# Starting the first query chunks on one token tile, with one reused transposing bank and the key weights loaded earlier

## The chip, the cores and the metric

The kernel runs on one core of a Trainium2 chip. The metric is the device time of one execution in microseconds (us). A profile accompanies every execution timed here: it gives the span (first to last instruction) and the mean granted TensorE clock, and for one execution per run a whole trace. Times in the traces are counted from the start of the span. "Fast" executions are those not marked as disturbed.

Engine names in the profile: PE is TensorE's matmuls, PEld its weight loads, DVE VectorE, ACT ScalarE, POOL GpSimd, SP SyncE. A small q after a name is that engine's sequencer or queue.

## The reference

Two layers, each an attention block A and a feed-forward block B, both with a residual, over 2048 tokens of width 1024 in bf16:

```python
x = A_x
for layer in range(2):               # written out twice in the original
    x = x + A(layernorm(x), wqkv, wo)        # 32 heads; token s attends to s, s-2, ..., s-14
    x = x + B(layernorm(x), w1, b1, w2, b2)  # gelu(x @ w1 + b1) @ w2 + b2, width 3584
```

(Condensed.) Only the first few steps matter here: the layernorm of the first 512 tokens (four tiles of 128), its transposition, and the first product, the queries `q = layernorm(x) @ Wq`.

## The kernel before

The kernel works on groups of 512 tokens. `qkv_chunk` computes 128 of the 1024 output columns for a group: eight matmuls (k = 0 to 7), each with a 128x128 piece of weights, whose columns are taken at a stride of eight (`c::NCH`), against up to 512 token columns. `acc_tile()` hands out one of the eight PSUM banks. In the traces the matmuls come in program order (after the change: 14 weight matmuls, 8 transposes, 42 weight matmuls, and so on as in the code), so a matmul that waits holds up those behind it.

The start loads tiles 0 and 1 of x, then the query weights in four pieces of two k each (512 KB), with x tiles 2 and 3 between them:

```python
load_x(0, 0, 2)
wq_first = [wpool.tile([P, KD // 2, D], BF16, name="wt") for _ in range(2)]
for k in range(0, KD, 2):
    load_wq_piece(wq_first[k // (KD // 2)], k)
    if k < 4:
        load_x(0, 2 + k // 2, 3 + k // 2)
```

Meanwhile TensorE runs warm-up matmuls on zeros. The layernorm of the first two tiles, and their transposition on TensorE (eight 128x128 transposes into a bank, then copies to SBUF), come as a pair:

```python
def ln_first():
    ...
    stats(0)
    stats(1)
    xn0 = norm(0)
    xn1 = norm(1)
    transpose_on_pe(xn0, xa[0][:, 0, :, :], parts=[act.copy] * 4)
    ps = transpose_bias()
    transpose_on_pe(xn1, xa[0][:, 1, :, :], parts=[vec.tensor_copy] * 2 + [act.copy] * 2)
    warm_up(2)
    act.copy(b1T[:], ps[:])
    stats(2)
    stats(3)
    for tt in range(2, 4):
        first_late.append((norm(tt), xa[0][:, tt, :, :]))
    ...
```

Then seven query chunks run over tiles 0 and 1 (256 columns), a quarter of the k at a time; the transposes of tiles 2 and 3 are put in between, and all chunks then take their other 256 columns:

```python
for kq in range(4 if n == 0 else 0):
    for c in range(7):
        first[c] = qkv_chunk(wq, c, xnT, first.get(c), kq * (KD // 4), (kq + 1) * (KD // 4), 0, 2)
        if (kq, c) == (2, 3):
            transpose_on_pe(*first_late.pop(0))
        if (kq, c) == (3, 4):
            ...
            transpose_on_pe(*first_late.pop(0))
            act.hold()
```

The layernorms of groups 1 and 2 (`ln_early`, eight tiles) follow on VectorE before its first attention products. The main program begins:

```python
warm_up(14)
ln_first()
build_constants()
with tc.tile_pool(name="early", bufs=1) as early:
    load_x(1)
    load_x(2)
    stage(gen_qkv(0, qk_next=early), sides=at(14, load_b2))
    ...
```

Of the kernel before, what the change touches and what calls it, by code (L numbers as in the profile page):

```python
# [17 lines left out]
def kernel(  # L18
# [18 lines left out]
    P = 128  # L37
# [100 lines left out]
    wq_first = [wpool.tile([P, KD // 2, D], BF16, name="wt") for _ in range(2)]  # L138
    for k in range(0, KD, 2):
        load_wq_piece(wq_first[k // (KD // 2)], k)  # L140
        if k < 4:
            load_x(0, 2 + k // 2, 3 + k // 2)

    warm = bigp.tile([P, P], BF16, name="big")
    vec.memset(warm[:], 0.0)
# [33 lines left out]
    def transpose_bias():  # L179
        ps = psum.tile([P, KF], BF16, name="acc", bufs=8)  # L180
        pe(nc.tensor.transpose(ps[:], b1_rows[:], ident[:KF, :KF]))  # L181
        return ps


    def ln_stats(t, mv=None, rstd=None):
        stats = lnp.tile([P, 2, 6], F32, name="stats")
# [7 lines left out]
        pool.tensor_tensor(out=rstd[:], in0=rstd[:], in1=mhalf[:], op=ALU.pow)  # L194
        return mv, rstd

    def ln_stats_ahead(g):
        junk = lnp.tile([P, D], BF16, name="xn", bufs=3)
        for tt in range(NTT):
            t, mean, var = g * NTT + tt, mv_ahead[:, tt, 0:1], mv_ahead[:, tt, 1:2]  # L200
            less = lnp.tile([P, 1], F32, name="less")
            act.activation(junk[:], x[t][:], ACT.Identity, scale=-1.0 / D, accum_out=less[:])
            act.activation(junk[:], x[t][:], ACT.Square, bias=less[:], accum_out=var)
            pool.tensor_scalar(out=mean, in0=less[:], scalar1=-1.0, scalar2=None, op0=ALU.mult)
            rstd = rstd_ahead[:, tt, :]
            pool.tensor_scalar(out=rstd, in0=var, scalar1=1.0 / D, scalar2=EPS, op0=ALU.mult, op1=ALU.add)
            pool.tensor_tensor(out=rstd, in0=rstd, in1=mhalf[:], op=ALU.pow)

    def ln_norm(t, mv, rstd, xn=None):
        if xn is None:  # L210
# [1 line left out]
        vec.tensor_scalar(out=xn[:], in0=x[t][:], scalar1=mv[:, 0:1], scalar2=rstd[:], op0=ALU.subtract, op1=ALU.mult)  # L212
        return xn

    def transpose_on_pe(xn, out, parts=None):
        pst = psum.tile([P, KD, P], BF16, name="acc", bufs=8)
        for k in range(KD):
            pe(nc.tensor.transpose(pst[:, k, :], xn[:, k * P:(k + 1) * P], ident[:]))  # L218
        parts = parts or [act.copy]
        n = KD // len(parts)  # L220
        for h, copy in enumerate(parts):
            copy(out[:, h * n:(h + 1) * n, :], pst[:, h * n:(h + 1) * n, :])
# [5 lines left out]
        xn = ln_norm(t, mv, rstd)  # L228
        last_transpose[0] = sp.dma_start_transpose(xnT[:, tt, :, :], xn[:].rearrange("s (k p) -> s k p", p=P))

    first_late = []

    def ln_first():

        xa[0] = new_xnT()
        vec.on = act.on = True
        mvs = {}
        stds = {}

        def stats(tt):  # L240
            st6 = lnp.tile([P, 2, 6], F32, name="stats")
            for h in range(2):
                vec.bn_stats(st6[:, h, :], x[tt][:, h * HALF:(h + 1) * HALF])
            mvs[tt] = lnp.tile([P, 2], F32, name="mv")
            vec.bn_aggr(mvs[tt][:], st6[:])
            stds[tt] = lnp.tile([P, 1], F32, name="std")
            act.activation(stds[tt][:], mvs[tt][:, 1:2], ACT.Sqrt, bias=eps_t[:])

        def norm(tt):
            rstd = lnp.tile([P, 1], F32, name="rstd")  # L250
            vec.reciprocal(rstd[:], stds[tt][:])
            return ln_norm(tt, mvs[tt], rstd)

        stats(0)
        stats(1)
        xn0 = norm(0)
        xn1 = norm(1)
        transpose_on_pe(xn0, xa[0][:, 0, :, :], parts=[act.copy] * 4)
        ps = transpose_bias()
        transpose_on_pe(xn1, xa[0][:, 1, :, :], parts=[vec.tensor_copy] * 2 + [act.copy] * 2)  # L260
        warm_up(2)
        act.copy(b1T[:], ps[:])
        stats(2)
        stats(3)
        for tt in range(2, 4):
            first_late.append((norm(tt), xa[0][:, tt, :, :]))
        vec.on = act.on = False
        act.hold()

    def new_xnT(pool=None):  # L270
        return (pool or xnp).tile([P, NTT, KD, P], BF16, name="xnT")
# [7 lines left out]
    xa = {}  # L279
    xb = {}  # L280

    def qkv_chunk(wts, c, xnT, ps=None, k0=0, k1=KD, t0=0, t1=NTT):
        if ps is None:
            ps = acc_tile()
        for k in range(k0, k1):
            mm(ps[:, t0 * P:t1 * P], lhsT=wts[k // (KD // 2)][:, k % (KD // 2), c::NCH], rhs=xnT[:, t0:t1, k, :],
               start=(k == 0), stop=(k == KD - 1), skip_group_check=t1 - t0 < NTT)
        return ps

    def add_prods(n):  # L290
# [13 lines left out]
            for _ in range(1 if c == 1 else 2):  # L304
                add_prods(n)

    def gen_qkv(n, defer=False, qk_pool=None, v_late=False, qk_next=None, v_first=False, mix=0):
        g = n % NG
        xnT = xa.pop(n)
        s = st[n]  # L310
        s["prods"] = []
        qk_pool = qk_pool or attp
        if v_first:
            wv = load_qkv(2)
        wq = wq_first if n == 0 else load_qkv(0)
        if not v_first:
            wk = load_qkv(1)

        def values():
            vT = attp.tile([P, NCH, HALO + T], BF16, name="vT", bufs=2)  # L320
            s["vT"] = vT
            act.on = n > 2
            act.copy(vT[:, :, 0:HALO], (zhalo if g == 0 else vhalo)[:])
            act.on = False
            for c in range(NCH):
                ps = qkv_chunk(wv, c, xnT)
                act.copy(vT[:, c, HALO:], ps[:])
                yield
            if g + 1 < NG:
                act.copy(vhalo[:], vT[:, :, T:T + HALO])  # L330

        if v_first:
            yield from values()
            wk = load_qkv(1)
        if n == 0:
            early_tiles = ln_early((1, None), (2, qk_next))
            for _ in range(NTT):
                next(early_tiles)
            wv = load_qkv(2)
            for _ in early_tiles:  # L340
                pass
            load_x(3)
        qT = qk_pool.tile([P, NCH, T], BF16, name="qT")
        first = {}
        for kq in range(4 if n == 0 else 0):
            for c in range(7):
                first[c] = qkv_chunk(wq, c, xnT, first.get(c), kq * (KD // 4), (kq + 1) * (KD // 4), 0, 2)
                if (kq, c) == (2, 3):
                    transpose_on_pe(*first_late.pop(0))
                if (kq, c) == (3, 4):  # L350
                    for done in range(2):
                        act.copy(qT[:, done, 0:2 * P], first[done][:, 0:2 * P])
                    transpose_on_pe(*first_late.pop(0))
                    act.hold()
        if n == 0:
            first[7] = qkv_chunk(wq, 7, xnT, t0=0, t1=2)
        for c in list(first)[2:]:
            act.copy(qT[:, c, 0:2 * P], first[c][:, 0:2 * P])
        kT = qk_pool.tile([P, NCH, HALO + T], BF16, name="kT")
        s["qT"], s["kT"] = qT, kT  # L360
        act.on = n > 2
        act.copy(kT[:, :, 0:HALO], (zhalo if g == 0 else khalo)[:])
        act.on = False

        def query(c):
            t0 = 2 if n == 0 else 0
            ps = qkv_chunk(wq, c, xnT, t0=t0)
            act.copy(qT[:, c, t0 * P:], ps[:, t0 * P:])

        def key(c):  # L370
            ps = qkv_chunk(wk, c, xnT)
            act.copy(kT[:, c, HALO:], ps[:])
            if not defer:
                new_prod(n, c)

        ahead = mix or NCH
        turns = [(query, c) for c in range(ahead)]
        for c in range(NCH):
            turns.append((key, c))
            if ahead + c < NCH:  # L380
                turns.append((query, ahead + c))
        for i, (chunk, c) in enumerate(turns):
            if i == NCH and n > 0 and not v_late and not v_first:
                wv = load_qkv(2)
            chunk(c)
            yield
        if g + 1 < NG:
            act.copy(khalo[:], kT[:, :, T:T + HALO])
        if not v_first:
            if v_late:  # L390
                wv = load_qkv(2)
            yield from values()
# [170 lines left out]
    def ln_early(*groups):  # L563
# [5 lines left out]
            tiles += [(n * NTT + tt, xns[:, tt, :], xa[n][:, tt, :, :]) for tt in range(NTT)]  # L569
        vec.on = True  # L570
        ahead = ln_stats(tiles[0][0])
        for i, (t, xn, xT) in enumerate(tiles):
            mv_rstd = ahead
            if i + 1 < len(tiles):
                ahead = ln_stats(tiles[i + 1][0])
            ln_norm(t, *mv_rstd, xn)
            sp.dma_start_transpose(xT, xn.rearrange("s (k p) -> s k p", p=P))
            if i + 1 == len(tiles):
                vec.on = False
            yield  # L580

    def stage(gen, count=None, sides=()):

# [19 lines left out]
    hold = vec.hold  # L603

    pool.on = True
    warm_up(14)
    ln_first()
    build_constants()
    with tc.tile_pool(name="early", bufs=1) as early:
        load_x(1)  # L610
        load_x(2)
        stage(gen_qkv(0, qk_next=early), sides=at(14, load_b2))
        q1 = gen_qkv(1, defer=True, qk_pool=early, mix=NCH // 2)
        stage(q1, sides=at(0, gather, 0) + at(11, between, 0, 1) + at(11, hold) + each(av, 0, 12, 1))
        q2 = gen_qkv(2, defer=True)
# [57 lines left out]
```

## Time and profile before

| what | before | view of the profile |
|---|---|---|
| time, median of 3 | 1230.84 us (1230.77 to 1231.01) | times |
| span of the profiled execution | 1229.1 us | page |
| TensorE busy | 1221.3 us, 99% | page, part 1 |
| first statistics on x tile 0 | 3.60 us | timeline |
| first transposes | 7.19 us | timeline |
| first matmul with weights | 8.95 us | timeline |
| first key matmul | 23.87 us | matmul starts in the trace |

Part 1 of the page of before has the busy time of each engine, its share of the span and its instructions; the line below it, from part 2, is the granted TensorE clock in 40 equal slices of the span (9 is 90% or more of full speed):

```profile
PE 1221.3 (99%) x5723; PEld 632.7 (51%) x5773; DVE 864.2 (70%) x918; ACT 315.1 (26%) x507; POOL 105.2 (9%) x209
...
PEclk9999999999999999999999999999999999999999
```

TensorE is the limit: 99% busy. (It has 5723 matmul records against 5773 weight loads, because some matmul records are missing from a trace.) The chain of waits of before, followed back from the last instruction and printed in order of time (start, length, what), tells where the other 1% is:

```profile
0.73 2.85 DMA x<-in_A_x_dram
...
3.60 1.30 DVE stats L92 x2
...
4.92 0.21 DVE mv L92
5.13 1.16 DVE stats L92 x2
...
6.58 0.56 DVE xn L92
...
7.19 0.62 PE acc L218 x8
...
8.95 4.12 PE acc L117 x36
```

Up to 7.19 us the chain is not TensorE: x arrives, VectorE computes the statistics of tile 0, then those of tile 1 (the 1.16 us at 5.13), and only then normalizes tile 0. The 1.16 us are the target of the change. The timeline of PE (start, length, engine and line, operation, output and input; in brackets the idle time before and what ended it) shows the same from the side of TensorE:

```profile
0.98 5.12 PE L117 MATMUL acc<-big 128*128 128x512 bf16 x14 [0.98 <-DVE big L92]
7.19 0.62 PE L218 MATMUL acc<-ident,xn 128*128 128x128 bf16 x8 [1.09 <-DVE xn L92]
...
8.31 0.59 PE L117 MATMUL acc<-big 128*128 128x512 bf16 x2
8.95 4.12 PE L117 MATMUL acc<-xnT,wt 128*128 128x256 bf16 x36
```

From 8.95 us on TensorE does not wait, except once for about 0.2 us near 125 us: one matmul of the output projection starts 415 ns after the one before it, where 512-column matmuls are otherwise 216 ns apart, because its input oT comes late from VectorE. The timeline has the wait at the load of its weights:

```profile
125.08 11.97 PEld L117 LDWEIGHTS <-oT 128*128 128x128 bf16 x56 [0.32 <-DVE oT L92]
```

VectorE itself works almost without a break from 28 us to there. Its two longer stops in that stretch, from the timeline of DVE in before:

```profile
28.60 6.69 DVE L92 TENSOR_TENSOR big<-qT,kT 128x4096 bf16<-128x4096 bf16 x3
...
90.65 4.50 DVE L92 TENSOR_TENSOR big<-abc,vT 128x4096 bf16<-128x4096 bf16 x2 [1.98 <-DMA abc<-a]
```

The first line is where it reaches its products of queries and keys (the stop of 0.71 us is just before, for a layernorm value from GpSimd); the second is a wait of 1.98 us for a DMA.

### The profile page before, as it was taken

What the parts mean: (1) busy time and instruction counts of PE and PEld (TensorE: products, weight loads), DVE (VectorE), ACT (ScalarE), POOL (GpSimd) and SP (SyncE); (2) the same over time, 40 slices, a digit from 0 to 9 for tenths busy, and PEclk for the clock granted to TensorE, in tenths of its full rate; (3) what the DMA queues carried; (4) which work ended last, traced back from release to release, by engine and by line L of the source; (5) the groups of instructions that cost most, each with busy time, mean ns of one, the idle gap of its engine ahead of it and who ended that gap; (6) DMA issues with size and microseconds to landing.
All of it is one profiled execution on the core that took longest, in us unless ns stands there. A gap on an engine that the chain in (4) does not pass through costs nothing.

```text
span 1229.1 us, 13953 instructions
## 1 busy us (share of the span) xinstructions
PE 1221.3 (99%) x5723; PEld 632.7 (51%) x5773; DVE 864.2 (70%) x918; ACT 315.1 (26%) x507; POOL 105.2 (9%) x209
## 2 busy tenths in 40 slices
PE   9999999999999999999999999999999999999998
PEld 7666544456444564446544465444654444444444
DVE  8999896998997999375993759937599797011001
ACT  4343253014410144202441024410244001400310
POOL 3010015010101101100001000010000002000000
PEclk9999999999999999999999999999999999999999
DMA  9954674756648745856557565576664558446441
GB/s 299 293 205 154 178 238 153 201 171 206 215 133 239 188 151 167 235 169 181 155 160 233 171 171 175 155 222 202 171 199 145 189 195 203 155 160 195 154 136 52
DMA packets 220031, 226.64 MB, mean 184 GB/s; under 512 B 68194, under 2 KB 187136, under 8 KB 217920
## 3 DMA queue, kind: packets, MB, share of 16 engines
q1 hardware_dynamic: 214704, 208.69, 56.9%
q0 software_dynamic: 5264, 17.06, 3.6%
q8 instruction: 45, 0.74, 0.2%
q14 instruction: 18, 0.15, 0.0%
HBM read 189.01 MB, written 4.19 MB: 157 GB/s over the span
## 4 chain that ended last, share of the span: by engine, by line
PE 99%; DVE 0%; issue 0%; DMA 0%
PE acc L117 99%; DMA x<-in_A_x_dram 0%; DVE stats L92 0%; PE acc L218 0%; DVE xn L92 0%; DVE x L92 0%; DVE mv L92 0%; PE acc L181 0%; DVE rstd L92 0%
## 5 line engine op out<-in xcount | busy, mean ns | idle before, releaser
L117 PE MATMUL acc<-xnT,wt 128*128 128x512 bf16 (+1 forms) x3392 | 720.3, 375 | 0.1
L117 PEld LDWEIGHTS <-wt 128*128 128x128 bf16 x3392 | 400.8, 119 | 318.0 <-issue 0.5
L117 PE MATMUL acc<-wt,hT 128*128 128x512 bf16 (+1 forms) x1780 | 386.0, 376 | 2.1
L117 PEld LDWEIGHTS <-hT 128*128 128x128 bf16 x1820 | 178.1, 98 | 209.0
L92 DVE TENSOR_TENSOR big<-big 128x1024 bf16<-128x1024 bf16 (+2 forms) x184 | 244.7, 1358 | 2.2
L92 ACT ACTIVATE hT<-acc,b1T 128x512 bf16<-128x512 f32 x224 | 152.1, 687 | 325.1 <-PE acc L117 325.0
L92 DVE TENSOR_TENSOR big<-qT,kT 128x4096 bf16<-128x4096 bf16 x64 | 143.8, 2284 | 36.4 <-ACT kT L92 35.9
L92 DVE TENSOR_TENSOR tmp<-acc,b2bc 128x512 f32<-128x512 f32 x56 | 38.6, 689 | 161.6 <-PE acc L117 158.5
L92 DVE TENSOR_TENSOR big<-abc,vT 128x4096 bf16<-128x4096 bf16 x64 | 144.6, 2284 | 9.8 <-DMA abc<-a 7.4
L92 ACT CAST qT<-acc 128x512 bf16<-128x512 f32 (+1 forms) x72 | 38.2, 543 | 277.6 <-PE acc L117 277.6
L117 PE MATMUL acc<-wt,oT 128*128 128x512 bf16 x440 | 97.6, 379 | 0.5
L92 DVE BATCH_NORM_STATS2 stats<-x 128x6 f32<-128x512 bf16 x120 | 79.9, 680 | 3.7 <-DMA x<-in_A_x_dram 2.7
L117 PEld LDWEIGHTS <-oT 128*128 128x128 bf16 x448 | 43.8, 98 | 53.0 <-DVE oT L92 0.3
L92 DVE TENSOR_TENSOR x<-acc,big 128x512 bf16<-128x512 f32 (+1 forms) x9 | 5.7, 632 | 90.1 <-PE acc L117 90.0
L92 ACT CAST vT<-acc 128x512 bf16<-128x512 f32 x64 | 37.4, 585 | 100.9 <-PE acc L117 100.8
L92 POOL TENSOR_TENSOR rstd<-mv,eps_t 128x1 f32<-128x1 f32 x56 | 17.4, 311 | 527.5 <-DVE mv L92 527.5
L92 ACT CAST kT<-acc 128x512 bf16<-128x512 f32 x64 | 37.3, 585 | 68.7 <-PE acc L117 68.7
L92 DVE TENSOR_TENSOR x<-acc,x 128x512 bf16<-128x512 f32 x64 | 43.0, 672 | 4.9 <-PE acc L117 4.4
L92 DVE TENSOR_SCALAR xn<-x,mv,rstd 128x1024 bf16<-128x1024 bf16 x52 | 28.4, 546 | 19.9 <-POOL rstd L92 19.5
L92 DVE TENSOR_TENSOR x<-tmp,x 128x512 bf16<-128x512 f32 x56 | 38.6, 689 | 1.4
L92 POOL DMA_DIRECT2D big<-big x24 | 13.3, 563 | 212.8 <-DVE big L92 212.8
L92 POOL TENSOR_TENSOR rstd<-rstd,mhalf 128x1 f32<-128x1 f32 x56 | 30.9, 551 | 4.4
(63 smaller groups left out, 259.4 us busy)
## 6 DMA issues: line engine op xcount, KB each, us to landing
wt<-in_B_w_dram SPq DMA_DIRECT2D x56, 1024.0 KB, 5.8
wt<-in_B_w_dram SPq DMA_DIRECT2D x64, 896.0 KB, 4.9
wt<-in_A_wqkv_dram SPq DMA_DIRECT2D x46, 1024.0 KB, 5.7
wt<-in_A_wo_dram SPq DMA_DIRECT2D x16, 1024.0 KB, 5.3
abc<-a POOLq DMA_DIRECT2D x32, 256.0 KB, 4.7
big<-big POOLq DMA_DIRECT2D x24, 256.0 KB, 3.8
x<-in_A_x_dram SPq DMA_DIRECT2D x16, 256.0 KB, 5.7
out_dram<-x SPq DMA_DIRECT2D x31, 128.0 KB, 1.8
```

What stands on the lines that cost most here:

```text
L92: inst = f(*args, **kwargs)
L117: return pe(nc.tensor.matmul(*args, **kwargs))
```

## The change

Its intent is to fill the idle start. Tile 0 is normalized as soon as its own statistics are there, and the first query chunks begin with its 128 columns alone; tile 1 follows separately for the first four k, and from k = 4 on both run together as before. All transposes use one bank, so seven banks remain for seven chunks. The key weights Wk are queued ahead of the third group of x. Two of the eight early layernorm statistics move from VectorE to ScalarE. The bias transpose moves behind the first key chunk.

The core of the diff (cuts marked with `...`):

```diff
-        if k < 4:
-            load_x(0, 2 + k // 2, 3 + k // 2)
+        if k == 2:
+            load_x(0, 2, 4)
...
-    def ln_stats_ahead(g):
+    def ln_stats_ahead(g, t0=0):
+        act.on = g == 2
...
-    def transpose_on_pe(xn, out, parts=None):
-        pst = psum.tile([P, KD, P], BF16, name="acc", bufs=8)
+    def transpose_on_pe(xn, out, bank, parts):
+        pst = bank[:].bitcast(BF16).rearrange("p (k t) -> p k t", t=P)
...
+        bn(0, 0)
+        bn(0, 1)
+        aggr(0)
+        std(0)
+        bn(1, 0)
+        norm(0, 2)
+        bn(1, 1)
+        aggr(1)
+        transpose_on_pe(xns[0], xnT[:, 0, :, :], bank, [lambda *io: (act.copy(*io), std(1))] + [act.copy] * 3)
+        some(0, 1, 0)
+        norm(1, 2)
+        transpose_on_pe(xns[1], xnT[:, 1, :, :], bank, [vec.tensor_copy] + [act.copy] * 3)
+        some(0, 1, 1)
+        some(1, 2, 0)
+        some(1, 2, 1)
...
+        some(0, 2, 2)
+        transpose_on_pe(xns[2], xnT[:, 2, :, :], bank, [act.copy])
+        norm(3)
+        some(0, 2, 3, range(4))
+        transpose_on_pe(xns[3], xnT[:, 3, :, :], bank, [act.copy] * 4)
...
+        load_x(1)
+        s["wk"] = load_qkv(1)
+        load_x(2)
...
+        on_act = tiles[-2:]
+        tiles = tiles[:-2]
...
-    warm_up(14)
-    ln_first()
-    build_constants()
...
-        load_x(1)
-        load_x(2)
-        stage(gen_qkv(0, qk_next=early), sides=at(14, load_b2))
+        warm_up(13)
+        build_constants()
+        begin_first(early)
+        stage(gen_qkv(0), sides=at(0, transpose_bias) + at(1, ln_stats_ahead, 2, NTT - 2) + at(3, ln_end) + at(6, load_b2))
```

`some(t0, t1, kq, chunks)` runs the quarter kq of the k of seven chunks (or of those named) over tiles t0 to t1 - 1; `norm(t, 2)` normalizes in two halves.

## The prediction

> **What bounds it.** TensorE: busy 99% of the span (page, part 1), 98.8% of the chain of waits is matmuls of the one helper line, granted clock 1.00. By the timeline, matmul starts from 15.6 us on lose only about 0.2 us to waiting (at 124.7 us, for oT from VectorE, which the timeline shows working almost without a break from 28.6 us to there). So only the first 16 us can be won; the rest is 512-wide matmuls, 215.7 ns apart.
>
> **Before, the start.** Tile 0's layernorm waits for tile 1's statistics; transposes start at 7.19 us, first real matmul at 8.95, then 128 matmuls 256 wide, 109.3 ns apart (Q half chunk 0.875 us), no waits. First K matmul about 23.9 us.
>
> **What the change does, costed.**
> 1. Tile 0 alone: normalization starts about 0.8 us earlier (one statistic of 0.6 and one aggregate fewer before it), in halves. Transposes from about 6.25 us; first real matmul, after the first 0.37 us copy, at about 7.4 instead of 8.95. The two late warm-ups (0.43) go.
> 2. It adds matmuls: the first four k of tiles 0 and 1 separately, 56 of 128 columns in place of 28 of 256. Their weights are taken every 8th element, 16 bytes apart; the Trainium skill ("SBUF — State Buffer", the note on 16-byte cachelines in the section on the DMA port swizzle) says that each new line costs. The trace agrees that they are slower: strided loads take 143 ns, contiguous ones 98. A 128-wide transpose has 56 ns spacing, as the skill's N/2.4+2.5 ns gives ("TensorE: Matmul & The Clock Gate", Back-to-back issue gap); but where a strided load starts together with a transpose the next matmul comes 8 to 9 ns late. I estimate 65 ns: 42 exposed ones cost 2.7 us against 3.1 for the 28, plus 0.9 for tile 0's first fourteen, hidden in the wait for tile 1. Net +0.6 us of TensorE work.
> 3. One bank serves all transposes, so transposes wait for copies of the tile before: tile 1 about 0.2 us (ScalarE's fourth copy, about 8.4), tile 3 about 0.4 (1.01 us copy of tile 2 against 0.875 us of matmuls), then 0.15 for tile 3's last copy.
> 4. Chunk 7 is 512 wide whole: no gain. Bias transpose moves into steady state: +0.1 us.
> 5. Wk lands earlier (about 20 instead of 22 us), but TensorE did not wait for it: nothing. Weights of Q land at 6.7, 9.0, 10.8, 12.2 us, in time.
> 6. Two statistics (1.85 us each in VectorE's cadence) leave VectorE; it then waits for kT, nets about 1.2 us, and the 0.2 us wait at 124.7 goes.
>
> Sum: earlier start -1.55, work +0.6, tile 1's transposes now behind it +0.45, waits +0.75: first K matmul about 24.1 us (+0.2); bias +0.1, oT wait -0.2: about +0.1 us.
>
> **Predicted: 1230.9 us**, 1230.1 to 1231.9. Faster by over 2%: 0.01; within 2%: 0.98; slower: 0.01.
>
> **What would show it.** First x-weight matmul at 7.4; 128-wide weight matmuls 65 ns apart; waits of about 0.2 and 0.4 us before the transposes of tiles 1 and 3; first K matmul near 24.1; no oT wait near 124; no wait for Wk.
>
> **What would make it wrong.** 128-wide spacing of 56 (-0.4 us) or 100 ns (+1.5); VectorE needing more than is freed, so that the oT wait grows; ScalarE's statistics delaying kT; the sparse start letting the clock fall to half (+1 to 2 us).

## The result, and the profile after

| | median (range) of its executions | before in the same rounds | ratio of fast means |
|---|---|---|---|
| changed kernel, first measurement | 1231.95 us (1231.18 to 4648.16), 6 | 1230.95 us, 6 | 1.0007 (95%: 0.9993 to 1.002) |
| changed kernel again | 1231.08 us (1231.06 to 1231.9), 5 | 1230.81 us, 9 | 1.0003 (95%: 0.999 to 1.0017) |

A ratio is the mean time of one kernel's fast executions over that of the other's of the same rounds, so it is not quite the ratio of the medians quoted. The best estimate is a loss of 0.4 to 0.8 us, and the intervals include no loss at all.

One execution took 4648.16 us. Its trace is of the first measurement. Timeline of PE, changed kernel, slow execution:

```profile
0.98 10.76 PE L117 MATMUL acc<-big 128*128 128x512 bf16 x13 [0.98 <-DVE big L92]
11.42 2.00 PE L219 MATMUL acc<-ident,xn 128*128 128x128 bf16 x8
```

From the third warm-up on, most 512-column matmuls start 840 ns apart, the others mostly 680 (840 ns is 0.61 columns per ns, about a quarter of the 2.37 of full clock), and they never recover, while the mean granted clock is given as 1.000 for the whole span of 4646.0 us. This is not a measurement: the trace holds no clock event at all, its page has no PEclk row, and the views count time without an event as full clock. Up to there both kernels run the same program on TensorE, warm-ups on zeros, and no other of about a hundred executions did it. So it is not put down to the change. The Trainium skill ("TensorE: Matmul & The Clock Gate", section "Seeing it yourself") warns that this clock has been seen stuck at a quarter and that its records cannot be fully trusted. This trace agrees with the first by its spacing of 840 ns, and with the second in that no event tells of it.

The profile after is therefore taken from the second measurement (1231.08 us, span 1228.9 us). Part 1 of its page, and its clock:

```profile
PE 1224.2 (100%) x5790; PEld 632.6 (51%) x5790; DVE 862.4 (70%) x913; ACT 319.1 (26%) x511; POOL 111.9 (9%) x211
...
PEclk9999999999999999999999999999999999999999
```

(PE's 1224.2 us against 1221.3 before is no measure of the change: the trace of before lacks 50 matmul records.) The chain of waits after, in order of time:

```profile
0.98 5.14 PE acc L117 x13
6.12 0.57 PE acc L219 x8
...
6.71 0.37 ACT xnT L92
...
7.10 0.29 ACT std L92
7.40 0.81 ACT xnT L92 x3
...
8.25 0.61 PE acc L219 x8
8.86 4.07 PE acc L117 x56
```

The layernorm has left the chain. In its place stand the warm-ups (which in this execution end just as tile 0 becomes ready) and ScalarE's copies out of the one bank. The timeline of PE after:

```profile
5.96 0.72 PE L219 MATMUL acc<-ident,xn 128*128 128x128 bf16 x8
7.14 1.01 PE L117 MATMUL acc<-xnT,wt 128*128 128x128 bf16 x14 [0.46 <-ACT xnT L92]
8.25 0.61 PE L219 MATMUL acc<-ident,xn 128*128 128x128 bf16 x8
...
14.47 0.61 PE L219 MATMUL acc<-ident,xn 128*128 128x128 bf16 x8 [0.22 <-ACT xnT L92]
14.91 10.52 PE L117 MATMUL acc<-xnT,wt 128*128 128x256 bf16 x78
25.37 0.18 PE L181 MATMUL acc<-ident,abc 28*128 28x28 bf16 x1
```

The first weight matmul starts at 7.14 instead of 8.95 us. But the first key matmul starts at 23.55 instead of 23.87 us: of 1.81 us gained, 0.32 are left. And 0.30 of those came from x, which happened to arrive earlier (first statistics at 3.30 instead of 3.60). Counted from the first statistics, the first weight matmul comes at 3.84 instead of 5.35 us, the first key matmul at 20.25 instead of 20.27: nothing left. Counted in the same way, the start of the last matmul comes at 1222.33 instead of 1222.18 us: 0.15 us behind.

The timeline of DVE after answers for the relief of VectorE:

```profile
26.17 4.49 DVE L92 TENSOR_TENSOR big<-qT,kT 128x4096 bf16<-128x4096 bf16 x2
...
64.35 2.29 DVE L92 TENSOR_TENSOR big<-qT,kT 128x4096 bf16<-128x4096 bf16 x1 [0.92 <-ACT kT L92]
...
90.27 4.50 DVE L92 TENSOR_TENSOR big<-abc,vT 128x4096 bf16<-128x4096 bf16 x2 [2.01 <-DMA abc<-a]
```

VectorE reaches its products 2.43 us earlier (26.17 for 28.60) and is 0.38 us earlier at 90 us (90.27 for 90.65); of both, 0.30 us is again the earlier arrival of x. Between, it waited 0.92 us for a key chunk that it did not wait for before.

### The profile page after: what moved, and what is told of

Its sections match the earlier page's. It is cut to its first block, busy times and chain, and to the rows that moved or that the text cites. A ratio compares the mean times of both kernels' runs of the same rounds, so it can differ in the third digit from the quotient of the medians.

```text
span 4646.0 us, 14040 instructions
## 1 busy us (share of the span) xinstructions
PE 4641.5 (100%) x5790; PEld 1327.2 (29%) x5790; DVE 869.0 (19%) x913; ACT 322.7 (7%) x511; POOL 107.5 (2%) x211
## 4 chain that ended last, share of the span: by engine, by line
PE 100%; DMA 0%; SPq 0%; DVE 0%; issue 0%
PE acc L117 100%; DMA wt<-in_A_wqkv_dram 0%; DMA x<-in_A_x_dram 0%; PE acc L219 0%; SPq L92 0%; DVE x L92 0%; PE acc L181 0%
## 5 line engine op out<-in xcount | busy, mean ns | idle before, releaser
L117 PE MATMUL acc<-xnT,wt 128*128 128x512 bf16 (+2 forms) x3412 | 2735.6, 1084 | 0.5 <-DMA x<-in_A_x_dram 0.5
L117 PE MATMUL acc<-wt,hT 128*128 128x512 bf16 (+1 forms) x1820 | 1473.7, 1091 | 0.0
L117 PEld LDWEIGHTS <-wt 128*128 128x128 bf16 x3412 | 800.7, 236 | 1928.5 <-issue 1917.8
L117 PEld LDWEIGHTS <-hT 128*128 128x128 bf16 x1820 | 403.7, 222 | 1068.6 <-issue 1068.6
L117 PE MATMUL acc<-wt,oT 128*128 128x512 bf16 x448 | 369.8, 1104 | 0.0
L117 PEld LDWEIGHTS <-oT 128*128 128x128 bf16 x448 | 99.3, 222 | 268.7 <-issue 268.7
L92 ACT CAST qT<-acc 128x512 bf16<-128x512 f32 x64 | 37.5, 586 | 1295.2 <-PE acc L117 1295.2
L92 DVE TENSOR_SCALAR xn<-x,mv,rstd 128x1024 bf16<-128x1024 bf16 (+1 forms) x54 | 28.6, 532 | 422.1 <-DMA xnT<-xn 412.7
L117 PE MATMUL acc<-wt,qT 128*128 128x512 bf16 x64 | 52.8, 1102 | 0.0
L92 POOL DMA_DIRECT2D abc<-a x32 | 17.6, 559 | 1197.7 <-DVE a L92 1197.7
```

What stands on the lines that cost most here:

```text
L92: inst = f(*args, **kwargs)
L117: return pe(nc.tensor.matmul(*args, **kwargs))
```

## The experiments

All kernels gave correct results and were timed over five rounds (the first measurement over six executions); all traced executions but that of the first measurement were fast. Each table entry is a mean over fast executions. "After the span" is the time less the span.

| kernel | time, us | span, us | after the span, us | before, same rounds | ratio (95%) |
|---|---|---|---|---|---|
| changed, first measurement | 1231.82 | 1229.64 | 2.18 | 1231.00 | 1.0007 (0.9993 to 1.002) |
| after_again | 1231.25 | 1229.08 | 2.17 | 1230.86 | 1.0003 (0.999 to 1.0017) |
| start_only | 1232.08 | 1230.16 | 1.92 | 1230.86 | 1.001 (0.9997 to 1.0022) |
| rest_only | 1230.77 | 1228.96 | 1.81 | 1230.86 | 0.9999 (0.9987 to 1.0012) |
| warm10 | 1232.74 | 1230.58 | 2.16 | 1231.28 | 1.0012 (0.9999 to 1.0024) |
| warm16 | 1232.00 | 1229.84 | 2.16 | 1231.28 | 1.0006 (0.9993 to 1.0018) |
| bias_gap | 1231.18 | 1229.38 | 1.80 | 1231.28 | 0.9998 (0.9984 to 1.0011) |
| better | 1232.70 | 1230.90 | 1.80 | 1231.28 | 1.0011 (0.9999 to 1.0024) |
| before_w0late | 1231.18 | 1229.40 | 1.78 | 1231.00 | 1.0001 (0.9988 to 1.0014) |
| after_w0late | 1233.19 | 1231.02 | 2.17 | 1231.00 | 1.002 (1.0006 to 1.0033) |
| small_late | 1231.46 | 1229.28 | 2.18 | 1231.00 | 1.0003 (0.9991 to 1.0016) |
| better2 | 1230.95 | 1229.18 | 1.77 | 1231.00 | 0.9999 (0.9987 to 1.0012) |
| one_more_act | 1232.05 | 1229.86 | 2.19 | 1231.06 | 1.001 (0.9996 to 1.0023) |

### The two halves of the change alone

The first question was which half costs. `after_again` is the changed kernel unedited:

> The changed kernel once more, unchanged, to get a trace of the fast state and more times. Theory of the prediction (the early start is eaten by narrow matmuls and by waits for the one bank): 1231.0 to 1231.8 us; in the trace the first weight matmul near 7.4 us, 128-wide weight matmuls 65 ns apart, waits of about 0.2 and 0.4 us before the transposes of tiles 1 and 3, first K matmul near 24.1 us. Rival (the sparser start lets the matrix engine fall back to half clock in some executions): times spread by more than 1 us, and in the trace some 512-wide or 256-wide matmuls after 6 us at twice their spacing. If the single 4648 us execution belongs to the kernel and not to chance, another one comes.

Its result is given above. `start_only` keeps the new start and leaves the rest as in before (all early layernorms on VectorE, Wk behind the third group of x):

```diff
         load_x(1)
-        s["wk"] = load_qkv(1)
         load_x(2)
+        s["wk"] = load_qkv(1)
...
-        on_act = tiles[-2:]
-        tiles = tiles[:-2]
...
-sides=at(0, transpose_bias) + at(1, ln_stats_ahead, 2, NTT - 2) + at(3, ln_end) + at(6, load_b2)
+sides=at(0, transpose_bias) + at(6, load_b2)
```

> The new start alone; all eight early layernorms on VectorE and Wk behind the third x group, as before. Theory: the start costs about 0.3 us (first K matmul +0.2, bias transpose +0.1) and VectorE is not relieved, so it reaches oT as before or up to 0.2 us earlier and the wait near 124 us stays at 0 to 0.3 us: 0.3 to 0.5 us slower than before. Rival (the statistics and Wk cost, the start gains): faster than before by 0.3 us or more.

`rest_only` is before with the other half, the earlier Wk and the two statistics on ScalarE:

```diff
         load_x(1)
+        st[0]["wk"] = load_qkv(1)
         load_x(2)
-        stage(gen_qkv(0, qk_next=early), sides=at(14, load_b2))
+        stage(gen_qkv(0, qk_next=early), sides=at(9, ln_stats_ahead, 2, NTT - 2) + at(11, ln_end) + at(14, load_b2))
```

> The old start; only Wk ahead of the third x group and two statistics on ScalarE. Theory: the one wait of 0.2 us near 124 us goes, nothing else changes for TensorE: 0.1 to 0.3 us faster than before, i.e. about 1230.7 us. Rival (ScalarE's statistics delay kT or the Wk load, which costs): slower than before by 0.3 us or more.

Measured: start_only 1232.08 us, rest_only 1230.77, before 1230.86 in the same rounds. The halves differ by 1.3 us, though one execution of start_only at 1233.96 us makes 0.5 of that (without it its mean is 1231.61). Each interval includes no change, and the two overlap, so this only suggests that what loss there is goes with the new start. The relief and the earlier Wk are worth nothing within what can be told: rest_only's matmuls of the output projection wait 0.04 us for oT instead of 0.2, and its key matmuls wait for no weights, and neither did before's. In start_only, which has no relief, the wait for oT is 0.01 us, so the wait can shrink without the relief. TensorE arrived later there (start of the first key copy 26.00 us against 25.48), and so did VectorE.

The timeline of PE in start_only shows one more thing about starts:

```profile
0.98 5.72 PE L117 MATMUL acc<-big 128*128 128x512 bf16 x13 [0.98 <-DVE big L92]
6.50 0.75 PE L219 MATMUL acc<-ident,xn 128*128 128x128 bf16 x8
```

All 13 warm-ups ran cold, 427 ns apart, and the transposes could not begin before 6.50 us. In after_again the warm-ups quicken to 216 ns apart at about 5.5 us. Over the traces that moment lies between 4.1 and 6.8 us, in kernels with the same warm-ups. So how long a fixed number of warm-ups takes is itself a matter of chance.

### The number of warm-ups

Since the new chain begins with the warm-ups, fewer of them might let the transposes start earlier. `warm10` and `warm16` change the one number:

```diff
-        warm_up(13)
+        warm_up(10)        # warm16: warm_up(16)
```

> The changed kernel with 10 warm-up matmuls in place of 13. In the two fast traces of the new start the clock rose to full at 5.5 us in one and at 6.8 us in the other; in the second, thirteen half-clock warm-ups of 427 ns lasted until 6.50 us and held back the transposes, which the data allowed at about 5.9. Theory (the late clock makes the warm-ups themselves the limit of the early start, in some executions): 10 of them end by 5.3 us in any case, so 0.2 to 0.4 us faster than the changed kernel on average, and the spread of its times shrinks below 1 us. Rival (the clock has nothing to do with it, the times scatter for other reasons): same mean and spread as the changed kernel; or fewer warm-ups let the clock rise later still: slower by 0.5 us.

> The changed kernel with 16 warm-ups. Theory: they end at 6.0 us when the clock rises early and near 7.2 us when it rises late, so transposes start 0.1 to 1.2 us after the data is there: 0.4 to 1.0 us slower than with 10. Rival: no difference between 10, 13 and 16.

warm10 took 1232.74 us, 1.5 more than before in its rounds, and the opposite of an improvement. The windows view shows why. Its columns: stretch, length, busy time (and instructions) of PE, PEld, DVE, ACT and POOL, granted clock, DMA share, GB/s. warm10:

```profile
5.00:6.00 1.00, 0.00 (x0) 0.00 (x0) 0.94 (x4) 0.29 (x1) 0.00 (x0) 1.00 0.81 186
...
7.00:8.00 1.00, 0.54 (x7) 0.46 (x6) 0.60 (x3) 0.87 (x4) 0.00 (x0) 0.63 1.04 398
8.00:9.00 1.00, 1.00 (x13) 1.00 (x11) 0.74 (x2) 0.60 (x3) 0.00 (x0) 0.50 1.05 399
9.00:10.00 1.00, 1.00 (x12) 1.00 (x11) 0.00 (x0) 0.00 (x0) 0.00 (x0) 0.50 1.05 401
```

and the same stretches of after_again:

```profile
5.00:6.00 1.00, 1.00 (x6) 0.30 (x4) 0.96 (x4) 0.16 (x1) 0.00 (x0) 1.00 1.08 397
...
7.00:8.00 1.00, 0.86 (x14) 0.86 (x13) 0.60 (x4) 0.98 (x5) 0.00 (x0) 1.00 1.06 402
8.00:9.00 1.00, 0.90 (x16) 0.85 (x15) 0.39 (x3) 0.20 (x1) 0.00 (x0) 1.00 1.05 397
9.00:10.00 1.00, 1.00 (x20) 1.00 (x19) 1.00 (x3) 0.70 (x3) 0.00 (x0) 1.00 1.04 389
```

With TensorE idle from 4.7 to 6.4 us, the granted clock was at half from 7.26 to 10.68 us by its record, and the 128-column matmuls came 107 ns apart instead of 60, from 7.6 us on. The theory that fewer warm-ups are better fell. Its other executions had mean clocks of 0.997 to 1.000 and spans of 1229.4 to 1232.5 us, so the fall comes in some executions and not in all. The Trainium skill ("TensorE: Matmul & The Clock Gate", section "What's actually happening") describes a window of 3413 ns that does not reset with the kernel, and a return to half clock after an idle window. This trace agrees with the length: 3.41 us at half clock, and 3.41 us at full clock before it. But in those 3.41 us, from 3.85 us on, TensorE was not idle; by the windows view it was busy for 1.58 us, 0.72 of them with transposes. So a partly idle stretch was enough. The other traces with a record of the clock narrow it down: in the 3.41 us after the clock first rose, PE was busy for 1.33 us in `better`, whose clock fell too, and for 1.72 us or more in the eleven whose clock stayed. Without the transposes it is 0.86 and 0.49 us against 1.12 or more, so the traces do not tell which of the two counts.

warm16, with more, took 1232.00 us and lost no clock: it was not slower than warm10, so that expectation missed too. In its trace the transposes came 2.83 us after the first statistics instead of 2.66. Neither number beat 13.

### The bias transpose in a gap

In after_again the two key matmuls around the bias transpose start 701 ns apart in three steps (312, 115 and 274 ns) where two steps of 216 would do: it costs 0.27 us in the steady state. `bias_gap` puts it into the wait between tile 0's transposes and its first weights, into the warm-ups' bank, and lets VectorE copy it:

```diff
     def transpose_bias():
-        ps = psum.tile([P, KF], BF16, name="acc", bufs=8)
-        pe(nc.tensor.transpose(ps[:], b1_rows[:], ident[:KF, :KF]))
-        act.copy(b1T[:], ps[:])
+        ps = warm_ps[0][:].bitcast(BF16)[:, :KF]
+        pe(nc.tensor.transpose(ps, b1_rows[:], ident[:KF, :KF]))
+        vec.tensor_copy(b1T[:], ps)
...
         transpose_on_pe(xns[0], xnT[:, 0, :, :], bank, [lambda *io: (act.copy(*io), std(1))] + [act.copy] * 3)
+        transpose_bias()
         some(0, 1, 0)
```

> The changed kernel with the bias transpose moved from between the first K chunks into the 0.6 us in which the matrix engine waits for the first copy of tile 0 (it writes into the bank of the warm-ups, VectorE copies it out). In the trace of the changed kernel that transpose cost 312-216 + 115 + 274-216 = 0.27 us between the chunks, not the 0.1 predicted. Theory: 0.2 to 0.3 us faster than the changed kernel, all of it visible as the second K chunk's distance from the first. Rival (VectorE's copy delays tile 1, which waits): no gain.

1231.18 us: level with before in its rounds (1231.28). From the first key copy to the last matmul's start its trace has 1199.79 us, against 1200.16 in after_again, so the cost is gone where it was (of the 0.37 us, 0.27 are the bias transpose and 0.10 the wait for oT, which this trace lacks). But the trace also shows a new wait, on the PE timeline of bias_gap:

```profile
7.33 0.18 PE L181 MATMUL acc<-ident,abc 28*128 28x28 bf16 x1 [0.33 <-DMA abc<-in_B_b_dram]
8.42 1.08 PE L117 MATMUL acc<-xnT,wt 128*128 128x128 bf16 x14 [0.91 <-DMA wt<-in_A_wqkv_dram]
```

The first piece of query weights arrived at 8.37 us here, against 6.63 in after_again. Nothing in the edit touches that transfer.

`better` combines bias_gap, 10 warm-ups and an interleaving of chunks 0 and 1 (against the 0.06 us stops at tile 3's copies):

```diff
-            else:
+            elif c == 0:
+                for kq in range(4):
+                    some(2, 4, kq, [0, 1])
+            elif c > 1:
                 for kq in range(4):
                     some(2, 4, kq, [c])
...
-        warm_up(13)
+        warm_up(10)
```

> 10 warm-ups, the bias transpose in the gap, and the last quarters of chunks 0 and 1 interleaved, so that chunk 1 fills the 0.17 us in which chunk 0 waits for the last two copies of tile 3. Theory: the three add up to 0.6 to 0.8 us against the changed kernel, so about 1230.4 us and 0.3 to 0.6 us faster than before as well. Rival (what is won at the start is lost again at the wait for oT near 124 us, which hangs on VectorE's chain from the K chunks on): the oT wait grows by as much, no gain over before.

1232.70 us: a miss, with the same fall to half clock in its trace (at half from 8.0 to 11.4 us by its record).

### When the first weights arrive

The arrival of the first weight piece differs from execution to execution. In the ten traces with tile x2 queued behind at least the first piece it landed at:

| kernel | landed, us | first weight matmul, us |
|---|---|---|
| before | 6.71 | 8.95 |
| after_again | 6.63 | 7.14 |
| start_only | 7.00 | 7.70 |
| rest_only | 7.35 | 9.15 |
| warm10 | 6.49 | 7.54 |
| warm16 | 7.48 | 7.53 |
| bias_gap | 8.37 | 8.42 |
| better | 8.13 | 8.18 |
| better2 | 8.33 | 8.37 |
| one_more_act | 7.04 | 7.10 |

A landing is counted in 16 steps. In each of these traces 9 to 14 of the 16 had come by 6.0 us, and the last came 0.5 to 2.4 us after that. At that time the queue is full: the windows view of before and of after_again has 373 to 404 GB/s in every us from 6 us on, with a DMA share of about 1.0. Before does not use the piece until 8.95 us, so a late landing costs it nothing. The changed kernel wants it at about 7.1 us.

To test whether this matters, `before_w0late` and `after_w0late` queue x tiles 2 and 3 ahead of the first piece, which delays it in both:

```diff
 wq_first = [wpool.tile([P, KD // 2, D], BF16, name="wt") for _ in range(2)]
+load_x(0, 2, 4)
 for k in range(0, KD, 2):
     load_wq_piece(wq_first[k // (KD // 2)], k)
-    if k == 2:             # in before: if k < 4, one tile each
-        load_x(0, 2, 4)
```

> The same exchange of loads in the kernel before, whose first weight matmul is at 8.95 us. Theory: it has slack for it, first weight matmul stays near 9.0 us, within 0.2 us of the kernel before. Rival (late weights cost any start the same): 0.5 to 0.9 us slower than before.

> The changed kernel with both loads of x tiles 2 and 3 ahead of the first piece of Wq, so that this piece lands about 1.3 us later (0.5 MB at 390 GB/s). In nine traces of the same first loads it landed between 6.5 and 8.4 us by itself. Theory (the early start needs this piece at 7.1 to 7.5 us, inside the range of its arrival, so arrival sets the start in some executions): first weight matmul near 8.3 us instead of 7.1 to 7.5, kernel 0.5 to 0.9 us slower than the changed kernel. Rival (the start is set by layernorm, copies and clock alone): within 0.2 us of the changed kernel.

In the traces the piece landed at 8.70 us in before_w0late and at 8.20 in after_w0late. Before did not mind (1231.18 us against 1231.00, ratio 1.0001, and its first weight matmul at 8.76 us; in its trace a key matmul waits 0.15 us for its weights at 24.87 us, which is new). The changed kernel took 1233.19 us, ratio 1.002 with an interval of 1.0006 to 1.0033, the only one that leaves out 1. The PE timeline of after_w0late:

```profile
8.24 1.09 PE L117 MATMUL acc<-xnT,wt 128*128 128x128 bf16 x14 [1.39 <-DMA wt<-in_A_wqkv_dram]
```

So the new start depends on a landing that the old one did not. Two of its five executions, at 1234.2 us, also had a mean clock of 0.999: an idle start seems to cost a second time, through the clock; only their mean clock is on record. The loss is more than the 0.5 to 0.9 us expected; without these two executions the mean span (1230.33 us) is 1.0 us above that of the changed kernel.

`small_late` asked whether GpSimd's two small transfers (the bias rows and a mask) make the late shares. They are issued after about 15 us instead of in the first 4:

```diff
-        pool.dma_start(mask[0::NTT, :, :], first[:])
+        return first
...
-    pool.dma_start(b1_rows[:], B_b1.rearrange("(j p) -> j p", p=P))
+    def load_b1():
+        pool.dma_start(b1_rows[:], B_b1.rearrange("(j p) -> j p", p=P))
```

> The changed kernel with GpSimd's two small DMAs (the rows of b1 and the mask, 7 and 12 KB) issued after 15 us instead of at 1.4 and 3.6 us. In the late executions one to six of the 16 DMA engines deliver their part of the first piece of Wq 1 to 3 us after the others, at the time of these two. Theory A (they hold those engines up): that piece lands by 7.0 us, and the changed kernel gets 0.2 to 0.5 us faster on average. Theory B (the stragglers have another cause): no change in mean or spread, and a landing after 7.2 us is as likely as before (4 of 9 traces).

1231.46 us, as the changed kernel. Its piece landed at 6.80 us in the trace, and its five spans lie closely together (1229.0 to 1229.7), but so few executions cannot tell that from chance. What delays the late shares stays open.

`better2` is `better` with the 13 warm-ups back:

> The changed kernel with its 13 warm-ups, the bias transpose in the gap of the start and chunks 0 and 1 interleaved at their last quarters. It differs from the run with 10 warm-ups alone, in which the granted clock fell to half for 3 us. Theory (13 warm-ups keep the clock up; the two edits save 0.27 and 0.17 us): clock full after the first rise, 0.3 to 0.5 us faster than the changed kernel, about level with before or up to 0.3 us faster. Rival (the clock falls in any start this sparse): granted clock near 0.5 between 7 and 11 us in the trace, and 1232 us or more.

1230.95 us against 1231.00 for before in the same rounds, ratio 0.9999. It is level, with the lowest single time of all the new kernels (1230.28). In its trace the weights were late again (landed at 8.33 us, an idle time of 1.44 us before the first weight matmul; the view puts it down to ScalarE's copy, but the first copy had ended by 7.3 us). So there is no version here that beats before by an amount that these rounds can show.

### The time after the last instruction

The spans do not explain all of the measured loss. Over the 36 executions of before in four batches the mean time is 1231.05 us and the mean span 1229.28; over the ten fast ones of the changed kernel they are 1231.53 and 1229.36. Of 0.48 us, 0.08 are in the span. (With the five executions of one_more_act, below, which differs by one tiny instruction, the mean span of the changed kernel is 1229.53, 0.25 more than before; the spans scatter by about that much.) The other 0.4 lie after the last instruction: time less span is 1.72 to 1.83 us in every one of those 36 executions of before, and 2.10 to 2.23 in every fast one of the changed kernel, without overlap. rest_only, bias_gap, better, better2 and before_w0late are of the short kind; warm10, warm16, small_late and after_w0late of the long kind; start_only lies at 1.84 to 2.06. The batches ran on four chips, and before is short and the changed kernel or its like long on each of them, so it is not the chip. What sets it is not the changed start, since bias_gap has that and is short.

The short and the long kinds differ in how many instructions each engine has; in all long ones up to then VectorE has 897 and ScalarE 493 by the built programs (913 and 511 on the pages of their profiles, and in no short one either number). `one_more_act` adds one tiny ScalarE instruction to the changed kernel:

```diff
     act.activation(one[:], eps_t[:], ACT.Sqrt)
+    act.activation(one[:], eps_t[:], ACT.Sqrt)
```

> This is the changed kernel with one more tiny ScalarE instruction at the start (the square root of one column is taken twice), so that ScalarE has 494 instructions instead of 493 and nothing else moves. It tests where 0.35 us of the measured loss lies. In the traces the time less the span (first to last instruction) is 2.16 to 2.22 us for the changed kernel and those built from it with 493 ScalarE and 897 VectorE instructions, and 1.74 to 1.85 us for before and the other kernels; the spans of the changed kernel average 1229.36 us and those of before 1229.26. Theory: this tail hangs on ScalarE's instruction count in some way (493 is bad, 489, 492, 497 and 501 are not). Then time less span falls to about 1.8 us here and the mean time by 0.35 us, to about 1231.0, with the span unchanged at about 1229.3 (1228.9 to 1230.4). Rival: it hangs on VectorE's count, or on something else that this edit leaves alone. Then time less span stays at 2.15 to 2.22 us and the mean time at about 1231.4.

Time less span stayed at 2.11 to 2.22 us. The theory of ScalarE's count fell. VectorE's count, or anything else that bias_gap changes and this edit does not, is left; the cause is open.

## Why the prediction was right, and where it was off

The call, within 2%, was right, and so was its reason: TensorE starts earlier and gives it back in more and smaller matmuls (+0.32 us in after_again), in tile 1's transposes (+0.45) and in waits for the one bank (+0.79). This split is read from the traces; no run of the new start gave the transposes a second bank or kept the 256-column matmuls, so the shares were not tested one by one. The number was 1230.9 us with a range of 1230.1 to 1231.9. The first measurement has a median of 1231.95 us over all six executions (1231.78 over the five fast ones), the second one of 1231.08. Point by point, with times in after_again:

| step as predicted | predicted | measured |
|---|---|---|
| start of transposes after the first statistics | 2.65 us | 2.66 us |
| first weight matmul, against before | -1.55 us | -1.51 us (3.84 for 5.35, from the first statistics) |
| spacing of 128-column weight matmuls | 65 ns | 60 ns |
| added TensorE work | +0.6 us | +0.32 us (2.53 for the 42, 0.85 for the first fourteen, less 28 x 109.3 ns) |
| tile 1's transposes now behind | +0.45 us | +0.45 us (8 x 56 ns) |
| waits for the reused bank | 0.2, 0.4, 0.15 us | 0.27, 0.38, 0.14 us |
| first key matmul, against before | +0.2 us | -0.02 us, from the first statistics |
| bias transpose in the steady state | +0.1 us | +0.27 us |
| wait for oT near 125 us | -0.2 us | -0.1 us in this trace (317 and 415 ns, where 216 is free); none left in one_more_act |
| wait for Wk | none before, none after | none |
| sum within the span | +0.1 us | +0.15 us in this pair of traces, +0.08 in the means |

That the sum came so close is partly luck: the start came out 0.22 us better than costed, the bias transpose and the wait for oT together 0.27 us worse. Four things were off.

- Step 2 was too dear: the 128-column matmuls with weights at a stride of eight come 60 ns apart, not 65. The reading of the Trainium skill that led there ("SBUF — State Buffer", note on 16-byte cachelines in the section "Door 1: The DMA port swizzle") fits in direction only: the transposes, with contiguous weights, come 56 ns apart, so what is left for the stride to explain is at most 4 ns per matmul; no run took the same weights without the stride. The same skill's sustained figure of about 81 ns for 128 columns with weight loads ("TensorE: Matmul & The Clock Gate", section "Back-to-back issue gap") is too high for both.
- Step 4 was too cheap: the bias transpose costs 0.27 us, because its neighbours start late as well (312 and 274 ns), and not only its own 0.1.
- Step 6, "nets about 1.2 us, and the 0.2 us wait at 124.7 goes", did not hold in after_again. VectorE's lead of 2.43 us at 26 us was down to 0.38 us at 90 us, after a wait of 0.92 us for a key chunk at 64 us that is new; and the wait for the DMA at 90 us stayed (2.01 for 1.98 us). A relief ahead of a wait for something else is given to that wait. The wait itself differs between executions: in one_more_act, which differs by one tiny instruction, it was gone as predicted. rest_only (relief alone, a wait of 0.04 us) and start_only (no relief, 0.01 us) suggest that its length follows when TensorE arrives as much as when VectorE does.
- Step 5, "Weights of Q land [...] in time", took the landing of one trace of before for a fixed time. In after_again it held (6.63 us), but in bias_gap, better and better2 the first piece landed 1.0 to 1.3 us after the 7.1 us at which the new start wants it, and in after_w0late forcing that cost 1.7 us in the mean span (1231.02 for 1229.36).

Two things were not in the prediction at all: the 0.4 us after the last instruction, which by the means is most of the measured loss, and that execution at quarter clock. The fall to half clock was named as a risk; in the changed kernel itself it was not seen, but with three fewer warm-ups it came in some executions.

## What to carry to other kernels

An idle start of 1.5 us on the limiting engine is worth what is left after the work that fills it: splitting matmuls of 256 columns (109 ns) into two of 128 (60 ns each), transposing the second tile in between and sharing one bank gave all of it back, the waits for the bank the most, so cost the smaller pieces before the idle time is counted as a gain. An earlier start also moves the first use of a transfer closer to its landing: look at the landing in several executions, not at one trace, and keep the clock in mind before idle or warm-up time is cut. And when a difference is below a us, split the time into the span and what lies after the last instruction, because here a part that no engine's work explains was larger than the part that was designed.

## What the Trainium skill lacked or had wrong

- "TensorE: Matmul & The Clock Gate", section "Back-to-back issue gap", gives about 81 ns for N = 128 and about 131 ns for N = 512 as the sustained spacing of matmuls with a weight load each. Here it was 60 ns with strided and 56 ns with contiguous weights for 128 columns, and 215.7 ns for 512; what the section calls the isolated gap (N/2.4 + 2.5 ns) fits the transposes and the 512-column matmuls of this sustained stream.
- The same page, section "What's actually happening", gives half clock "after ≥1 idle window". In warm10 the clock fell at 7.26 us although PE had been busy for 1.58 us of the 3.41 us before (0.86 without the transposes); with 1.72 us (1.12 without) or more it stayed. The section does not say how idle a window must be.
- The same page, section "Seeing it yourself", has the clock stuck at a quarter for 50 us and more. Here it was one execution of over a hundred, for its whole span of 4646.0 us, with no clock event in the trace.
- "SBUF — State Buffer", note on 16-byte cachelines: no figure for weight loads. Here matmuls of 128 columns whose weights lie 16 bytes apart were spaced 4 ns wider than transposes with contiguous ones (60 against 56), though a load itself is recorded as much longer (143 against 98 ns).
- "Runtime: NRT & Kernel Launch", section "The ~15µs preamble/postamble breakdown", lists fixed times around a kernel. Here the time less the span had two levels that went with the kernel, 1.72 to 1.84 and 2.10 to 2.23 us, with one kernel at 1.84 to 2.06; the page tells of no such levels, and what sets them the runs did not show.
- "DMA: Bandwidth & Descriptors", section "Latency and other measured facts", calls two of the 16 engines usually slower (its guess at a cause is for software-generated descriptors, and these transfers ran on the hardware queue), but does not tell how far the shares of one transfer spread when the queue is full. Here 9 to 14 of the 16 steps of the landing of a 512 KB piece had come by 6.0 us and the last between 6.5 and 8.4 us.
